# The last stage's product with both halves of w_out as one 512-column matmul, the second sum at eviction, and another order of the first stages' instructions

## The chip, the cores and the metric

The kernel runs on one core of one Trainium2 chip. The metric is the device time of one execution in microseconds; lower is better. Several executions are timed, and their median is given. One more execution is recorded by the profiler.

## The reference

Attention of 2048 tokens (4 x 8 heads, 512 tokens of width 64) with 32 state rows a head, in both directions, then two feed-forward layers over the 2176 rows. Everything is float32.

```python
def _attn_ref(x, state):
    scores = scale * np.matmul(x, state.transpose(0, 1, 3, 2))
    a = softmax(scores); xread = np.matmul(a, state)
    scores2 = scale * np.matmul(state, x.transpose(0, 1, 3, 2))
    a2 = softmax(scores2); sread = np.matmul(a2, x)
    return np.concatenate([xread, sread], axis=2)

def _moe_ref(x, w_in, w_out):          # 2304 x 512, 512 x 2048, 2048 x 512
    h = x @ w_in
    g = np.where(h >= 1, h, np.where(h <= -1, 0.0, (h + 1) ** 2 / 4.0))
    return g @ w_out

def _moe2_ref(x, w_a, w_b, w_out):     # 512 x 1536 twice, 1536 x 512
    return (x @ w_a * (x @ w_b)) @ w_out
```

(softmax stands here for the maximum, exponential and sum of the reference, cut.)

## The kernel before

**Precision.** TensorE multiplies in a format that holds fewer bits than float32. Most operands are therefore split into a high half, a copy by ScalarE (`hi_of`, line 351), and a low half, a subtraction by VectorE (`split`, lines 358 to 362). A product of two split operands takes three matmuls: high x high, high x low, low x high (`three`, line 377). `mms` (line 364) issues them, all under line 371.

**Stages.** The first (`phase_one`, line 1332) does the attention and the first layer's h = x @ w_in. The softmaxes are taken in groups of heads; the state is multiplied into w_in first (`w_steps`, line 650, matmuls under line 660 into the banks 6 and 7, "upper"), and the softmax weights then multiply the result in 64 units of six 512-column matmuls (`h_mm`, line 799; unit t is row f of w_in's columns for the heads' group j). `gate` (line 775) applies the activation and a store writes g to DRAM. The weights come from DRAM as 8-byte numbers; `conv_steps` (line 390) turns them into float32 with a copy (line 423), a ScalarE conversion (line 346) and a VectorE join (line 434). The second stage (`b_steps`, line 952) multiplies g by w_out in three chunks of tokens. The third (`ab_run`, line 1131) forms a * b. The last stage multiplies p = a * b by the second layer's w_out, called u here.

**The last stage.** 128 tokens are done plainly (`o_plain`, line 1250), the other 2048 in eight runs of 256 (`o_run`, line 1267). A run is one step of Strassen and Winograd's scheme: seven products of half-size blocks in place of eight. A block of p is 128 tokens by 6 rows f of 128; a block of u is 6 rows f of 128 by HC = 256 columns. `sp` splits a block of p into one of eight slots (`aslot`), after sums and differences of blocks by VectorE (`v_sum`, line 900). `product` (line 1282) issues 6 x 3 matmuls of 256 columns into the first half of a bank; products 6, 7 and 4 add onto the bank of product 1, and 3 onto that of 5. `post` (from `sums`, line 858) evicts the bank behind each product: for 1, 5, 6 and 4 a ScalarE copy into the output block (`act`, line 346), for 2, 3 and 7 a VectorE addition to it (`tt`, line 356). The order of products on TensorE is 1, 7 of the run before, 5, 2, 4 of the run before, 6, 3; the last run ends with 6, 7, 3, 4. The halves of u lie one behind the other (`uv`, line 1215).

**The order of the instructions** is written by a planner (`Flow`, line 20). `op` records each instruction in the order of its creation, with the engines that may run it, a cost, and what it reads and writes. `order` (line 85) walks forward in its own time and gives each engine the ready instruction with the earliest due time (`late`). TensorE's instructions are taken in the order of creation (`chain`), except those marked `loose`, which may run when they are ready. A bank counts as taken by whoever reads or writes it. DMAs are issued on SP's queue in the planner's order.

Of the kernel before, what the change touches and what calls it, by code (L numbers as in the profile page):

```python
# [16 lines left out]
DRAM = bass.MemoryType.DRAM  # L17


class Flow:  # L20
# [13 lines left out]
    def __init__(self):  # L34
        self.ops = []
        self.last = {}
        self.readers = {}
        self.loose = set()
        self.gate = None
        self.hold = None  # L40
        self.row = None
        self.rush = 0.0
        self.port = set()
        self.hurry = {}

# [39 lines left out]
    def order(self):  # L85
# [32 lines left out]
        late = [x - self.hurry[i] for i, x in enumerate(late)]  # L118
        free = dict.fromkeys(self.LAT, 0.0)
# [15 lines left out]
        for _ in range(n):  # L135
# [40 lines left out]
            for s in after[i]:  # L176
                left[s] -= 1
                when[s] = max(when[s], free[e] if (e,) == (*ops[s][0],) and not ops[i][3] else fin[i])
                if not left[s]:
                    offer(s)  # L180
# [6 lines left out]
def attention_then_two_mlps(  # L187
# [189 lines left out]
    def three(w, x):  # L377

        return [(w[0], x[0]), (w[0], x[1]), (w[1], x[0])]
# [266 lines left out]
    def w_state(*args):  # L646
        for f in w_steps(*args):
            f()

    def w_steps(b, n, f0=0, f1=4):  # L650
# [4 lines left out]
        def emit(e):  # L655
            for j in range(4):
# [17 lines left out]
                loose=b == 0 and n > 0,  # L674
# [540 lines left out]
    def uv(i, h):  # L1215
        return V2("R0", USL[i] + 4 * UF * HC * h, UF, HC, HC)
# [50 lines left out]
    def o_run(t0, final=False):  # L1267
# [12 lines left out]
        post = sums(*bk, HC, (o0.sub(0, HC), o0.sub(HC, HC), o1.sub(HC, HC), o1.sub(0, HC)))  # L1280

        def product(i):
            u = [uv(i, h) for h in range(2)]

            def pairs():
                out = []
                for f in range(UF):
                    out += three([v()[:, f, :] for v in w[i]], [v()[:, f, :] for v in u])
                return out

            mms(bk[TO[i]], HC, pairs, i in "125", True, 3 * UF, regs(*w[i], *u), i in "3674")
            post[i]()
# [39 lines left out]
    def phase_one():  # L1332
# [39 lines left out]
        for b, (soft, tr, read, after) in enumerate(TIMES):  # L1372
# [3 lines left out]
            if b < 3:  # L1376
                if b:
                    PLAN.setdefault(16 * b - 5, []).append((st_load, b + 1))
                PLAN[soft].append((lambda b: (a_load(2 * b), a_load(2 * b + 1)), b + 1))
                PLAN.setdefault(after, []).extend([(b_qk, b + 1), (b_soft, b + 1)])  # L1380
        nv = 0
        for t in range(4 * F1):
# [8 lines left out]
            if j < 3 and f % 4 == 3:  # L1391
                w_state(j + 1, f // 4)
# [102 lines left out]

    order = flow.order()
# [81 lines left out]
```

## Time and profile before

| | |
|---|---|
| median of the runs | 720.42 us (719.61, 720.42, 723.85) |
| profiled execution | 719.44 us, its span on the core 717.3 us |
| TensorE busy | 699.2 us, 97% of the span, 4818 matmuls |
| VectorE busy | 559.3 us, 78% |
| ScalarE busy | 424.8 us, 59% |
| GpSimd busy | 97.3 us, 14%, all in the first stage |
| granted clock, mean | 0.998 |

Times in the rows are microseconds from the start of the span. PE is TensorE's matmuls, PEld its weight loads, DVE VectorE, ACT ScalarE, POOL GpSimd, SP the queue that issues DMAs. A tile's name stands without its number: `bank` is a bank of PSUM, `upper` the banks 6 and 7 together, `lower` 4 and 5, `f`, `fs`, `r` and `rh` are regions of SBUF. A matmul's recorded duration is longer than the time until the next one starts, since matmuls overlap.

### The profile page before, as it was taken

What the parts mean: (1) busy time and instruction counts of PE and PEld (TensorE: products, weight loads), DVE (VectorE), ACT (ScalarE), POOL (GpSimd) and SP (SyncE); (2) the same over time, 40 slices, a digit from 0 to 9 for tenths busy, and PEclk for the clock granted to TensorE, in tenths of its full rate; (3) what the DMA queues carried; (4) which work ended last, traced back from release to release, by engine and by line L of the source; (5) the groups of instructions that cost most, each with busy time, mean ns of one, the idle gap of its engine ahead of it and who ended that gap; (6) DMA issues with size and microseconds to landing.
All of it is one profiled execution on the core that took longest, in us unless ns stands there. A gap on an engine that the chain in (4) does not pass through costs nothing.

```text
span 717.3 us, 12235 instructions
## 1 busy us (share of the span) xinstructions
PE 699.2 (97%) x4818; PEld 655.4 (91%) x4818; DVE 559.3 (78%) x701; ACT 424.8 (59%) x625; POOL 97.3 (14%) x72
## 2 busy tenths in 40 slices
PE   7799999999999999999999999999999999999997
PEld 5456667989899999999999999999999999999997
DVE  6888879988998687899899786655636798987760
ACT  4787989797544446666566675655425535544440
POOL 3346555573100000000000000000000000000000
PEclk9999999999999999999999999999999999999999
DMA  9867967497466157143425767454541248454201
GB/s 346 357 214 245 357 236 272 149 349 250 147 200 242 35 162 219 50 141 138 133 99 203 226 203 243 157 167 135 183 163 42 87 150 279 127 188 136 87 30 44
DMA packets 75449, 128.92 MB, mean 180 GB/s; under 512 B 5632, under 2 KB 51200, under 8 KB 75392
## 3 DMA queue, kind: packets, MB, share of 16 engines
q1 hardware_dynamic: 75392, 128.15, 53.1%
q8 instruction: 37, 0.61, 0.4%
q14 instruction: 20, 0.16, 0.1%
HBM read 84.87 MB, written 43.25 MB: 179 GB/s over the span
## 4 chain that ended last, share of the span: by engine, by line
PE 82%; DVE 7%; DMA 5%; ACT 2%; issue 2%; POOL 1%; SPq 0%; DVEq 0%; POOLq 0%; ACTq 0%
PE bank L371 76%; DMA f<-in_w_dram 2%; PE bank L829 2%; DVE rh L356 2%; DMA p_d<-f 1%; DMA f<-p_d 1%; PE upper L660 1%; DVE r L356 1%; PE lower L758 1%; PE bank L853 1%; ACT f L346 1%; DVE fs L434 1%; DVE fs L549 1%; DVE fs L793 1%; ACT rh L346 0%
## 5 line engine op out<-in xcount | busy, mean ns | idle before, releaser
L371 PE MATMUL bank<-rh,r 128*128 128x352 f32 (+2 forms) x1398 | 223.5, 316 | 2.6 <-DVE rh L356 2.1
L371 PEld LDWEIGHTS bank<-rh,r 128*128 128x128 f32 x1398 | 215.8, 189 | 4.6 <-DVE rh L356 3.0
L371 PE MATMUL bank<-r,r 128*128 128x368 f32 (+1 forms) x960 | 156.1, 315 | 0.0
L346 ACT ACTIVATE f<-bank 128x368 f32<-128x368 f32 (+3 forms) x183 | 82.4, 453 | 119.3 <-PE bank L371 118.3
L371 PEld LDWEIGHTS bank<-r,r 128*128 128x128 f32 x960 | 147.9, 188 | 0.0
L346 ACT ACTIVATE rh<-f 128x736 fp32r<-128x736 f32 (+5 forms) x120 | 100.7, 846 | 77.7 <-PE bank L371 61.3
L356 DVE TENSOR_TENSOR rh<-f,rh 128x736 fp32r<-128x736 f32 (+5 forms) x120 | 120.2, 1014 | 26.1 <-ACT rh L346 25.6
L356 DVE TENSOR_TENSOR f<-bank,f 128x368 f32<-128x368 f32 (+2 forms) x168 | 85.6, 516 | 69.0 <-PE bank L371 64.0
L371 PE MATMUL bank<-r 128*128 128x512 f32 (+1 forms) x582 | 122.1, 362 | 2.8 <-ACT r L346 1.1
L371 PEld LDWEIGHTS bank<-r 128*128 128x128 f32 x582 | 95.5, 191 | 28.5 <-issue 5.1
L346 ACT ACTIVATE r<-f 128x768 fp32r<-128x768 f32 (+6 forms) x85 | 80.0, 952 | 40.8 <-PE bank L371 17.6
L356 DVE TENSOR_TENSOR r<-f,r 128x768 fp32r<-128x768 f32 (+6 forms) x85 | 91.9, 1090 | 15.7 <-ACT r L346 15.6
L371 PE MATMUL bank<-rh 128*128 128x352 f32 (+2 forms) x564 | 93.3, 318 | 0.5 <-DVE f L356 0.5
L904 DVE TENSOR_TENSOR f<-f 128x256 f32<-128x256 f32 (+7 forms) x108 | 85.8, 811 | 6.3 <-DMA f<-p_d 5.2
L371 PEld LDWEIGHTS bank<-rh 128*128 128x128 f32 x564 | 88.4, 189 | 1.4 <-issue 0.7
L371 PE MATMUL bank<-r,rh 128*128 128x368 f32 (+1 forms) x480 | 80.3, 315 | 0.0
L371 PEld LDWEIGHTS bank<-r,rh 128*128 128x128 f32 x480 | 74.3, 188 | 0.0
L346 ACT ACTIVATE f<-f 128x1024 fp8e5<-128x1024 f32 (+1 forms) x43 | 47.8, 1120 | 2.2 <-POOL f L423 2.0
L421 ACT ACTIVATE f<-f 128x512 fp8e5<-128x512 fp8e5 (+1 forms) x29 | 29.5, 1018 | 24.5 <-DMA f<-in_w_dram 18.4
L434 DVE SCALAR_TENSOR_TENSOR f<-f 128x1024 uint32<-128x1024 uint32 (+1 forms) x34 | 34.9, 1027 | 5.9 <-ACT f L346 5.8
L779 ACT ACTIVATE f<-bank,half 128x512 f32<-128x512 f32 x40 | 27.1, 686 | 8.1 <-PE bank L371 4.4
L793 DVE SCALAR_TENSOR_TENSOR f<-f,bank 128x512 f32<-128x512 f32 x40 | 26.3, 675 | 6.6 <-POOL f L788 4.0
(65 smaller groups left out, 425.9 us busy)
## 6 DMA issues: line engine op xcount, KB each, us to landing
f<-in_w_dram SPq DMA_DIRECT2D x25, 1024.0 KB, 6.2
f<-g_d SPq DMA_DIRECT2D x36, 368.0 KB, 5.5
f<-p_d SPq DMA_DIRECT2D x17, 768.0 KB, 5.0
g_d<-f SPq DMA_DIRECT2D x40, 256.0 KB, 4.3
f<-in_w_dram SPq DMA_DIRECT2D x18, 512.0 KB, 3.9
p_d<-f SPq DMA_DIRECT2D x48, 184.0 KB, 2.1
g_d<-fs SPq DMA_DIRECT2D x28, 256.0 KB, 3.6
f<-g_d SPq DMA_DIRECT2D x16, 352.0 KB, 4.5
```

What stands on the lines that cost most here:

```text
L346: lambda e: nc.scalar.activation(dst(), src(), func, **{k: (v() if callable(v) else v) for k, v in kws.items()}),
L356: op({"DVE": t_tt(n)}, lambda e: nc.vector.tensor_tensor(dst(), a(), b(), alu), rd, wr, port=port)
L371: nc.tensor.matmul(o, w, x, start=first and k == 0, stop=last and k == n - 1, skip_group_check=onto)
L421: nc.scalar.activation(to(), of(), AF.Copy, saturate=False)
L434: lambda e: nc.vector.scalar_tensor_tensor(out(U32), words_of(1, U32)(), 5, z(U32), ALU.logical_shift_right, ALU.bitwise_or),
L549: op({"DVE": 1.25}, lambda e: nc.vector.transpose(t1(), wide["lower"]), both, regs(t1))
L660: nc.tensor.matmul(banks[ab[q]][o : o + NS, :cols].rearrange("p (f x) -> p f x", x=P), st[q]()[64 * h : 64 * h + 64, NS * j : NS * j + NS] ...
L758: nc.tensor.matmul(banks[4][64 * e2 : 64 * e2 + 64, o : o + NS], xn()[:, c * 256 + p * 128 + e2 * 64 : c * 256 + p * 128 + (e2 + 1) * 64], ...
L779: lambda e: nc.scalar.activation(g(), h(), AF.Relu, bias=half[:, 0:1], scale=0.5),
L793: lambda e: nc.vector.scalar_tensor_tensor(g(), g(), 1.0, h(), ALU.min, ALU.max),
L829: nc.tensor.matmul(banks[b][:, P * i : P * i + P], w[:, P * c : P * c + P], xs()[:, P * c : P * c + P], start=c == 0, stop=c == 3,)
L904: lambda e: eng(e).tensor_tensor(dst(), a(), b(), alu),
```

## The change

In the last stage the two halves of u are laid side by side, so that a row f holds 512 columns: 256 of the high half and 256 of the low half. A product multiplies the high half of p by all 512 in one matmul, which fills a whole bank, and the low half of p by the first 256. The bank's upper 256 columns then hold high x low, and the eviction adds them: a ScalarE copy or a VectorE addition for the first half as before, and a VectorE addition for the second half, for each product.

In the first stage the products of state and w_in for the later groups of heads are created at other places (`AHEAD`), and all of them are loose. The planner takes numbers off the due times of 27 instructions (`NUDGE`, named by their number in the order of creation; a negative one makes it later), and two of them lose one of their engines.

```diff
+NUDGE = {
+    2: (2.5,), 3: (11,), 52: (11.5,), 58: (-12.5,), 62: (52.5,), 64: (53,), 65: (362,), 69: (-3.5,), 83: (-2,),
+    89: (-3,), 110: (4.5,), 137: (13, "POOL"), 163: (5.5,), 188: (-13,), 219: (-8.5,), 304: (7.5,), 328: (6, "ACT"),
+    1010: (32.5,), 1011: (5.5,), 1091: (-2.5,), 1103: (-1,), 1124: (-11.5,), 1138: (-6,), 1188: (-3.5,),
+    1211: (2.5,), 2330: (-4.5,), 2365: (9,),
+}
...
         late = [x - self.hurry[i] for i, x in enumerate(late)]
+        single = [len(e) == 1 for e, _, _, _ in ops]
+        for i, (x, *off) in self.nudge.items():
+            late[i] -= x
+            ops[i] = ({e: t for e, t in ops[i][0].items() if e not in off}, *ops[i][1:])
...
-                when[s] = max(when[s], free[e] if (e,) == (*ops[s][0],) and not ops[i][3] else fin[i])
+                when[s] = max(when[s], free[e] if single[s] and e in ops[s][0] and not ops[i][3] else fin[i])
...
-                loose=b == 0 and n > 0,
+                loose=b > 0 or n > 0,
...
     def uv(i, h):
-        return V2("R0", USL[i] + 4 * UF * HC * h, UF, HC, HC)
+        return V2("R0", USL[i] + 4 * HC * h, UF, 2 * HC, HC)
+
+    def uboth(i):
+        return V2("R0", USL[i], UF, 2 * HC, 2 * HC)
...
-        post = sums(*bk, HC, (o0.sub(0, HC), o0.sub(HC, HC), o1.sub(HC, HC), o1.sub(0, HC)))
+        c11, c12, c22, c21 = o0.sub(0, HC), o0.sub(HC, HC), o1.sub(HC, HC), o1.sub(0, HC)
+        post = {
+            "1": (0, c11, True),
+            "2": (1, c11, False),
+            "5": (2, c22, True),
+            "6": (0, c12, True),
+            "3": (2, c12, False),
+            "7": (0, c22, False),
+            "4": (0, c21, True),
+        }
+
+        def put(x, v, new):
+
+            def half(k):
+                return lambda: banks[bk[x]][:, HC * k : HC * k + HC]
+
+            for k in range(2):
+                if new and not k:
+                    act(v, half(k), HC, AF.Copy, [bank(bk[x])], regs(v))
+                else:
+                    tt(v, half(k), v, ALU.add, HC, [bank(bk[x])] + regs(v), regs(v))
 
         def product(i):
-            u = [uv(i, h) for h in range(2)]
+            b, first = bk[TO[i]], i in "125"
 
-            def pairs():
-                out = []
+            def emit(e):
                 for f in range(UF):
-                    out += three([v()[:, f, :] for v in w[i]], [v()[:, f, :] for v in u])
-                return out
-
-            mms(bk[TO[i]], HC, pairs, i in "125", True, 3 * UF, regs(*w[i], *u), i in "3674")
-            post[i]()
+                    hi, lo = (v()[:, f, :] for v in w[i])
+                    u = uboth(i)()[:, f, :]
+                    nc.tensor.matmul(banks[b], hi, u, start=first and not f, stop=False, skip_group_check=True)
+                    nc.tensor.matmul(
+                        banks[b][:, :HC], lo, u[:, :HC], start=False, stop=f == UF - 1, skip_group_check=True
+                    )
+
+            op({"PE": UF * (t_mm(512) + t_mm(HC))}, emit, regs(*w[i], *(uv(i, h) for h in range(2))), [bank(b)])
+            put(*post[i])
...
+        AHEAD = {7: [(1, 0)], 11: [(1, 1)], 15: [(1, 2)], 19: [(1, 3)], 22: [(2, 0)], 26: [(2, 1)], 30: [(2, 2)], 34: [(2, 3)], 38: [(3, 0)], 42: [(3, 1)], 45: [(3, 2)], 47: [(3, 3)]}
...
-            if j < 3 and f % 4 == 3:
-                w_state(j + 1, f // 4)
+            for b, n in AHEAD.get(t, ()):
+                w_state(b, n)
...
+    flow.nudge = NUDGE
     order = flow.order()
```

## Rows read from the trace of the kernel before

**Rows 1.** The page: span, and each engine's busy time, share and instructions.
```profile
span 717.3 us, 12235 instructions
...
PE 699.2 (97%) x4818; PEld 655.4 (91%) x4818; DVE 559.3 (78%) x701; ACT 424.8 (59%) x625; POOL 97.3 (14%) x72
```

**Rows 2.** Stretch; busy us (instructions) of PE, PEld, DVE, ACT, POOL; clock, DMA, GB/s.
```profile
20.00:30.00 10.00, 6.10 (x59) 3.21 (x60) 9.10 (x13) 7.95 (x13) 3.09 (x2) 0.89 1.02 408
...
28.30:31.50 3.20, 3.20 (x9) 2.48 (x9) 2.52 (x3) 3.20 (x7) 1.23 (x1) 0.54 1.02 406
...
40.00:60.00 20.00, 17.94 (x189) 11.10 (x189) 19.75 (x22) 15.86 (x21) 10.22 (x8) 1.00 0.75 241
```

**Rows 3.** Timeline: start, duration, instructions merged, count, idle time before and releaser.
```profile
54.36 1.09 PE L660 MATMUL upper<-fs 64*32 64x512 f32 x16 [1.26 <-DVE r L356]
...
185.60 2.28 PE L371 MATMUL bank<-rh,r 128*128 128x368 f32 x12 [0.75 <-DVE rh L356]
```

**Rows 4.** Busy time by stretch in the last stage, columns as in rows 2.
```profile
620.00:640.00 20.00, 20.00 (x171) 20.00 (x170) 18.39 (x26) 10.55 (x17) 0.00 (x0) 1.00 0.52 171
...
680.00:700.00 20.00, 20.00 (x171) 20.00 (x170) 13.64 (x17) 8.26 (x13) 0.00 (x0) 1.00 0.11 41
```

**Rows 5.** Timeline of TensorE: 512-column matmuls, first stage; 256-column ones, last stage.
```profile
121.38 0.50 PE L371 MATMUL bank<-r 128*128 128x512 f32 x1
...
121.71 5.40 PE L371 MATMUL bank<-r 128*128 128x512 f32 x23
...
126.72 0.39 PE L371 MATMUL bank<-r 128*128 128x512 f32 x1
...
698.21 4.42 PE L371 MATMUL bank<-r,r 128*128 128x256 f32 x36
...
702.47 2.32 PE L371 MATMUL bank<-rh 128*128 128x256 f32 x18
```

**Rows 6.** VectorE's instructions from 603.0 to 633.8 us: count, busy us, mean ns, idle.
```profile
L356 DVE TENSOR_TENSOR r<-f,r 128x768 fp32r<-128x768 f32 x13 | 11.9, 951 | 0.0
...
L356 DVE TENSOR_TENSOR rh<-f,rh 128x768 fp32r<-128x768 f32 x6 | 5.7, 952 | 0.2 <-ACT rh L346 0.2
L356 DVE TENSOR_TENSOR f<-bank,f 128x256 f32<-128x256 f32 x7 | 2.7, 417 | 0.0
```

**Rows 7.** Timeline: two evicting additions in a row.
```profile
626.51 0.75 DVE L356 TENSOR_TENSOR f<-bank,f 128x256 f32<-128x256 f32 x2
```

**Rows 8.** Timeline where run 1 of the last stage begins.
```profile
602.32 0.96 DVE L904 TENSOR_TENSOR f<-f 128x768 f32<-128x768 f32 x1 [2.83 <-DMA f<-p_d]
...
604.20 1.97 PEld L371 LDWEIGHTS bank<-rh,r 128*128 128x128 f32 x16 [0.26 <-DVE r L356]
```

**Rows 9.** Timeline of the end: product 7 after product 6, and the last copy.
```profile
706.95 0.38 ACT L346 ACTIVATE f<-bank 128x256 f32<-128x256 f32 x1 [1.74 <-PE bank L371]
...
707.39 2.39 PE L371 MATMUL bank<-rh,r 128*128 128x256 f32 x18 [0.47 <-ACT f L346]
...
714.03 0.38 ACT L346 ACTIVATE f<-bank 128x256 f32<-128x256 f32 x1 [6.70 <-PE bank L371]
```

**Rows 10.** Timeline from 20 to 28 us, VectorE's order ahead of the steady matmuls.
```profile
20.62 1.78 DVE L423 COPY f<-f 128x1024 uint8<-128x1024 uint8 x1
...
21.19 0.45 ACT L346 ACTIVATE r<-upper 128x128 fp32r<-128x128 f32 x2 [0.50 <-PE upper L660]
...
22.30 0.47 DVE L356 TENSOR_TENSOR r<-upper,r 128x128 fp32r<-128x128 f32 x2
...
22.69 1.21 DVE L695 TENSOR_REDUCE fs<-lower 128x2 f32<-128x1024 f32 x1
...
23.82 2.33 DVE L434 SCALAR_TENSOR_TENSOR fs<-f 128x1024 uint32<-128x1024 uint32 x2
...
26.07 0.74 DVE L356 TENSOR_TENSOR r<-upper,r 128x256 fp32r<-128x256 f32 x2
...
26.87 1.13 PE L660 MATMUL upper<-fs 64*32 64x512 f32 x16 [2.46 <-DVE r L356]
```

More of the change, by code (lines that the diff above doesn't have):

```diff
@@ L44, in __init__ @@
         self.hurry = {}
+        self.nudge = {}
     def op(self, engs, emit, rd=(), wr=(), size=0, loose=False, port=False):
```

## The prediction

> **What bounds the kernel now.** I read the page first: TensorE is busy for 97% of a span of 717.3 us, VectorE for 78%, and the chain that ended last runs over TensorE for most of its length [rows 1]. Busy time says little here, because matmuls overlap; what counts is the time from start to start, and where TensorE waits. So I next read the table of busy time by stretch. In the first stages TensorE is busy only 6.10 of 10 us from 20 to 30 us, its granted clock is 0.54 from 28.3 to 31.5 us (nearly all at the lower of its two levels, 1.2 GHz, where it was idle much of the time before), and from 40 to 60 us VectorE is busy 19.75 of 20 us [rows 2]. The timeline then shows single waits of TensorE: 1.26 us at 54.36, where the product of state and w_in for the next pair of heads stands in a fixed place and its two banks still wait for a VectorE subtraction, and 0.75 us at 185.60, one of two such within 4 us [rows 3]. From 190 us to the last stage TensorE streams almost without a gap. In the last stage VectorE has little room at first (18.39 of 20 us busy from 620 to 640) and much later (13.64 of 20 from 680 to 700) [rows 4]. So the last stage is paid in matmul time, as long as VectorE keeps up, and the first stages in waits.
>
> **The matmuls of the last stage.** Eight runs of seven products stream, for each of the six rows f of a product, 3 x 256 columns; after the change 512 + 256, the same 768. What is saved is the fixed part of one matmul, 8 x 7 x 6 = 336 times. The 36 matmuls of 256 columns from 698.21 to 702.47 stand 4.26/36 = 0.1183 us apart. Of 512 columns the trace has rows in the first stages: from 121.71 to the start of the 23rd at 126.72, 5.01/22 = 0.2277 us; with the one before, at 121.38, 5.34/23 = 0.2322 [rows 5]. So a row f goes from 3 x 0.1183 = 0.3549 to 0.2277 + 0.1183 = 0.3460, 8.9 ns less: 336 x 0.0089 = 3.0 us. Bounds: with 0.2322 it is 4.4 ns and 1.5 us; if one whole fixed part goes (0.1183 less 256 columns at 2.4 GHz, 0.1067, so 11.6 ns), 3.9 us. I take 3.0, since the 0.2277 comes from a steady stretch as the last stage is. Zero, where 512 columns cost just two matmuls of 256 (0.2366), is a rival below.
> The Trainium skill speaks against this (TensorE: Matmul & The Clock Gate, Back-to-back issue gap): a warm matmul costs its columns at 2.4 GHz and some 2.5 ns; by that, 336 fewer matmuls would give an estimated 0.8 us. The trace disagrees so far: 0.1183 and 0.2277 us lie 11.6 and 14.4 ns above the column time.
>
> **The second sum at the eviction.** Each product now ends with two evictions of 256 columns in place of one: the high half's product with the low half of w_out lies in the bank's upper 256 columns and VectorE adds it. The four products that ScalarE copied (1, 5, 6, 4) get an add behind the copy, the three that VectorE added (2, 3, 7) a second add: 56 more adds. One takes 0.417 us [rows 6], but two in a row 0.75 us [rows 7], so 0.33 to 0.42 each, 18.5 to 23.5 us of VectorE in all. What hides them is VectorE's idle time and its lead. From 603.0 to 633.8 us it made 13 + 6 = 19 low-half splits, beside the sums and 7 adds, with almost no idle time [rows 6]; TensorE used up 30.8/2.13 = 14 products in that time (2.13 us is half of the 4.26 above), two of them split before. So VectorE gained 7 products, some 7 x 30.8/19 = 11 us of its time. Fifteen more adds there take 5.0 to 6.3 us: the lead grows more slowly but does not go. From 680 on 10 more adds (4.2 us) fit in 6.4 us of idle time per 20. I charge 0.3 us for single late evictions; a bank's next product comes two or more products (4 us) later, but for the end of the last run.
> If the cover is gone, TensorE waits for splits as it does once now: at 604.20 its weight load waits 0.26 us for VectorE, whose sum began 2.83 us late because a load of p had not landed [rows 8]. That load also sets the start of run 1, so what the five products of run 0 before it save (5 x 6 x 8.9 ns = 0.27 us) is lost there: +0.3 us.
> **The end.** In the last run product 7 follows product 6 in the same bank: TensorE waits 0.47 us for ScalarE's copy, and the last instruction before the store is a copy of 0.38 us behind product 4 [rows 9]. Both now have an add behind them that needs the copy: 0.42 each, and a hand-over, which was 0.06 us from the copy's end at 707.33 to TensorE's start at 707.39: +0.47 twice, +0.9 us. No work covers either.
> Last stage: -3.0 + 0.3 + 0.3 + 0.9 = -1.5 us. The strided layout of the split w_out (steps of 512) moves no instruction and its 256-column pieces stay whole: nothing.
>
> **The order of the first stages.** Two edits, and none of them issues a DMA of its own. First, the twelve products of state and w_in for later heads are created up to four units later and are now all free to start when their banks are free, where they held a fixed place in TensorE's order. The wait at 54.36 [rows 3] is of that kind: TensorE can run the next unit instead. I take -1.0 of its 1.26 us, since VectorE is full there [rows 2] and part comes back as another wait; its bounds are 0 and -1.26.
> Second, 27 numbers shift due times. Counting creations in the code, 62 and 64 are the low subtractions of the second state product, moved ahead by 53 us; 52 is the copy for w_in rows 4 and 5, by 11.5; 65 is the maximum for the second softmax, by 362. In the trace that copy holds VectorE from 20.62 for 1.78 us, the two subtractions come after it at 22.30 though ScalarE had written their other operand by 21.64, then the maximum (1.21 us) stands in front of the two joins at 23.82, and behind those the subtractions at 26.07 release the matmuls at 26.87 that waited 2.46 us [rows 10]. Putting the subtractions first is worth 22.30 - 21.64 = 0.7 us, the maximum elsewhere 1.2 us less what it delays; I take -1.7 for both (bounds 0 and -1.9). The copy behind them is needed for the fourth unit only, some 5 us later. SP's queue changes little: the two first loads were first already. Two of the numbers also bind one instruction each to a single engine; I take nothing for it, since it moves work of 1 to 2 us between engines and removes none. The stretch at half clock right after costs half of 3.2 us x 0.92, some 1.5 us; it follows the idle time before it and may go with it (-1.5) or stay; I leave it in. Of the two waits from 185.60 on, and smaller ones that later numbers (1010 to 1211, third chunk) touch, I take -0.8 of 1.5, both ends 0 and -1.5.
> First stages: -1.7 - 1.0 - 0.8 = -3.5 us; ends 0 and -6.2 (1.9 + 1.3 + 1.5 + 1.5).
>
> **Sum.** The profiled execution took 719.44 us. 719.44 - 1.5 - 3.5 = 714.4. It lay 0.98 below the median of the runs, and below all three; I add half of that, 0.5, to each case: 714.9, said as 715.0.
>
> **Rivals** (from 719.44, with the 0.5).
> A. All first waits and the half clock go: -1.5 - 6.2, so 712.2; with the upper bound of the matmul term 711.3. For: the waits are VectorE's order, not its total, before 40 us. Against: 19.75 of 20 us from 40 to 60.
> B. The order gains nothing because VectorE's work is only permuted: 719.44 - 1.5 + 0.5 = 718.4.
> C. The change does not do what it says: 512 columns cost two of 256, nothing is saved, and adds and end remain (+1.5 with the 0.3 for run 1 left out: +1.2): 719.44 + 1.2 - 3.5 + 0.5 = 717.6. Against: [rows 5]. The rule of the Trainium skill above (same page and section) comes close to it: its estimated 0.8 us would make this case 716.8.
> D. VectorE is late in runs 1 to 3: the lead of 11 us was partly splits made early by putting adds off, and adds can be put off less now. Each of some 14 products would wait as at 604.20, about 0.3 us: +4.2, so 719.1. It decides when adds and the lost lead exceed 11 us.
> E. Slower: the copy of 1.78 us pushed behind the subtractions is late for the fourth unit; TensorE idles at 30 us instead of 26, and a second 3.2 us at half clock follows. +1.78 + 1.6 in place of -3.5, since the later stages start late too: 719.44 - 1.5 + 3.4 + 0.5 = 721.8. It decides when w_in's join comes after 31 us. Against: it has 5 us.
>
> **Numbers.** Forecast 0.37, A 0.20, B 0.14, C 0.10, D 0.12, E 0.07. Within 1% (7.2 us, about what a measurement of this kernel tells from no change) means 713.2 to 727.6. Faster by more: nearly all of A and a quarter of the forecast, whose own range is 712.5 to 717: 0.28. Slower by more: only E at double its price, 0.03. Same: 0.69. The range 710.0 to 721.0 goes 1.3 us under A's end, for waits too short to be listed here, and leaves out most of E.
>
> **What would show it.** Right: 336 fewer matmuls; rows of 512 columns in the last stage about 0.228 us apart from start to next start; 80 VectorE adds from the banks in place of 24; an idle time of about 0.9 us before product 7; the start of the steady stream at 26 instead of 28 us; no wait at 54. Wrong: waits of TensorE's weight loads for VectorE between 604 and 645 (D), the lower clock twice (E), a product of the last stage still 2.13 us long (C).

## The result, and the profile after

The median went from 720.36 us (719.61 to 723.85) to 713.0 us (711.8 to 713.18): a ratio of 0.9885, with an interval of 0.9851 to 0.9919. That is 7.4 us, where 715.0 and 5.4 us were forecast. The profiled execution of the changed kernel took 713.18 us, its span 711.3 us, 6.0 us less than that of before.

In the new numbering the lines up to the last stage stand 13 lines lower (L371 is now L384, L356 is L369, L346 is L359, L423 is L436, L434 is L447, L660 is L673, L758 is L771, L793 is L806, L904 is L917). The last stage's matmuls are L1325, of 512 columns, and L1326, of 256.

The page of after, its span and its engines (before: [rows 1]):

```profile
span 711.3 us, 11604 instructions
...
PE 695.4 (98%) x4482; PEld 638.2 (90%) x4482; DVE 575.0 (81%) x759; ACT 420.5 (59%) x620; POOL 104.6 (15%) x75
...
L369 DVE TENSOR_TENSOR f<-bank,f 128x368 f32<-128x368 f32 (+2 forms) x224 | 108.4, 493 | 69.9 <-PE bank L384 57.0
```

336 matmuls are gone (4818 to 4482). The last row is the group of VectorE additions from the banks; it holds 224. The same group on the page of before holds 168, so 56 were added, as the code says:

```profile
L356 DVE TENSOR_TENSOR f<-bank,f 128x368 f32<-128x368 f32 (+2 forms) x168 | 85.6, 516 | 69.0 <-PE bank L371 64.0
```

Busy time by stretch of after; the columns are those of [rows 2], and the stretches those of [rows 2, 4]:

```profile
20.00:30.00 10.00, 5.20 (x40) 1.99 (x40) 9.51 (x15) 8.04 (x12) 2.56 (x2) 0.84 1.02 408
40.00:60.00 20.00, 20.00 (x137) 13.02 (x136) 18.93 (x25) 16.57 (x26) 10.25 (x8) 1.00 0.83 290
...
620.00:640.00 20.00, 20.00 (x117) 17.50 (x116) 18.79 (x29) 8.93 (x15) 0.00 (x0) 1.00 0.33 107
680.00:700.00 20.00, 20.00 (x115) 17.28 (x113) 17.59 (x29) 7.59 (x13) 0.00 (x0) 1.00 0.08 31
```

TensorE lost time between 20 and 30 us (5.20 us busy after 6.10) and gained it from 40 to 60 (20.00 after 17.94). In the two stretches of the last stage it has no idle time although VectorE is busier (18.79 us after 18.39, and 17.59 after 13.64). Its weight loads, PEld, are busy 17.50 and 17.28 of 20 us there, after 20.00 and 20.00.

**Where the time came from.** The first 256-column matmul of the last stage starts at 578.86 us where it started at 583.56: 4.70 us are won before the last stage. From there to the start of the last matmul it is 128.45 us after 130.16, 1.71 less; from there to the end of the span 4.01 after 3.57, 0.44 more. 4.70 + 1.71 - 0.44 = 6.0. So most came from the order, not from the matmuls.

These are two executions, and executions differ. The eight runs of the last stage begin at 593.08 us in before and at 588.38 in after. In the six other profiled kernels below with the new order and its whole first-stage table (e0, e2, e5, e6, e7, e10) they begin at 586.70 to 588.84. So the order is worth 4.2 to 6.4 us by the traces, and 4.70 lies near the lower end. (e1, which has the order of before, begins them at 594.14.)

The 4.70 us are mostly waits of TensorE. Its idle time up to 580 us, added up over the stretches, fell from 14.22 to 11.28 us, by 2.9. A wait costs more than its idle time shows: before product 7 it made the product 1.09 us longer than the median (3.197 - 2.111) where its idle time is 0.93, since a recorded matmul reaches into the gap behind it. The part of the 4.70 that neither explains was not traced. Between 20 and 190 us the waits with a releaser fell from eleven to five.

The wait view of TensorE from 20 to 190 us, first of before and then of after (columns: group, releaser, us in total, times, longest):

```profile
PE upper L660 <- DVE r L356: 4.1, 3, 2.5
PE bank L371 <- DVE rh L356: 1.5, 2, 0.8
PE upper L660 <- DVE fs L434: 1.3, 1, 1.3
PE bank L371 <- DVE fs L793: 0.6, 1, 0.6
...
```

```profile
PE upper L673 <- DVE r L369: 4.6, 2, 4.4
PE lower L771 <- ACT fs L359: 0.7, 1, 0.7
PE bank L384 <- ACT r L359: 0.6, 1, 0.6
PE bank L384 <- DVE r L369: 0.4, 1, 0.4
```

The two waits for a split's low half, the pair from 185.60 on [rows 3], are gone, and so is that at 54.36. The product of state and w_in still waits, and in one place longer than before.

That place is the start. TensorE, VectorE and one row of ScalarE of after there (columns: start, us; before: [rows 10]):

```profile
20.36 0.49 DVE L369 TENSOR_TENSOR r<-upper,r 128x128 fp32r<-128x128 f32 x2
20.75 1.23 DVE L447 SCALAR_TENSOR_TENSOR fs<-f 128x1024 uint32<-128x1024 uint32 x1
...
23.80 0.42 DVE L369 TENSOR_TENSOR r<-upper,r 128x256 fp32r<-128x256 f32 x1
24.13 0.68 DVE L714 TENSOR_SCALAR fs<-fs 128x2 f32<-128x2 f32 x1
24.29 0.36 ACT L359 ACTIVATE r<-upper 128x256 fp32r<-128x256 f32 x1
24.87 0.75 DVE L436 COPY f<-f 128x1024 uint8<-128x1024 uint8 x1
25.51 1.21 DVE L447 SCALAR_TENSOR_TENSOR fs<-f 128x1024 uint32<-128x1024 uint32 x1
26.64 0.41 DVE L369 TENSOR_TENSOR r<-upper,r 128x256 fp32r<-128x256 f32 x1
...
27.11 1.96 PE L673 MATMUL upper<-fs 64*32 64x512 f32 x16 [4.41 <-DVE r L369]
29.00 3.58 PE L384 MATMUL bank<-r 128*128 128x512 f32 x12
```

The subtractions come at 20.36 instead of 22.30, as the prediction wanted. But the last subtraction that releases the next state product now stands behind a small instruction, a copy and a join, and ends at 27.05. ScalarE had written its other operand by 24.65. So the 2 us won ahead of it are lost again, and the stream begins at 29.00 instead of 27.93.

### The profile page after: what moved, and what is told of

Read it like the earlier page. It is cut to its first block, busy times and chain, and to the rows that moved or that the text cites. A ratio compares the mean times of both kernels' runs of the same rounds, so it can differ in the third digit from the quotient of the medians.

```text
span 711.3 us, 11604 instructions
## 1 busy us (share of the span) xinstructions
PE 695.4 (98%) x4482; PEld 638.2 (90%) x4482; DVE 575.0 (81%) x759; ACT 420.5 (59%) x620; POOL 104.6 (15%) x75
## 4 chain that ended last, share of the span: by engine, by line
PE 89%; DVE 4%; DMA 4%; ACT 1%; issue 1%; POOL 0%; DVEq 0%; POOLq 0%; ACTq 0%
PE bank L384 67%; PE bank L1325 11%; PE bank L1326 6%; PE bank L842 2%; PE upper L673 2%; DMA f<-in_w_dram 2%; DMA g_d<-fs 1%; PE lower L771 1%; DMA f<-g_d 1%; PE bank L866 1%; DVE fs L447 1%; ACT f L359 1%; DVE f L436 0%; DVE r L369 0%; PE lower L539 0%
## 5 line engine op out<-in xcount | busy, mean ns | idle before, releaser
L384 PE MATMUL bank<-rh,r 128*128 128x352 f32 (+2 forms) x1074 | 181.8, 326 | 1.0 <-DVE rh L369 1.0
L384 PEld LDWEIGHTS bank<-rh,r 128*128 128x128 f32 x1074 | 176.3, 188 | 1.9 <-DVE rh L369 1.6
L359 ACT ACTIVATE f<-bank 128x368 f32<-128x368 f32 (+3 forms) x183 | 82.7, 454 | 141.8 <-PE bank L384 90.2
L369 DVE TENSOR_TENSOR f<-bank,f 128x368 f32<-128x368 f32 (+2 forms) x224 | 108.4, 493 | 69.9 <-PE bank L384 57.0
L359 ACT ACTIVATE rh<-f 128x736 fp32r<-128x736 f32 (+5 forms) x120 | 100.3, 846 | 71.6 <-PE bank L384 63.4
L369 DVE TENSOR_TENSOR rh<-f,rh 128x736 fp32r<-128x736 f32 (+5 forms) x120 | 119.0, 1001 | 22.2 <-ACT rh L359 21.8
L384 PE MATMUL bank<-r,r 128*128 128x368 f32 x672 | 120.6, 330 | 0.0
L384 PEld LDWEIGHTS bank<-r,r 128*128 128x128 f32 x672 | 113.1, 188 | 0.1
L384 PE MATMUL bank<-r 128*128 128x512 f32 (+1 forms) x438 | 102.0, 385 | 2.4 <-ACT r L359 1.2
L369 DVE TENSOR_TENSOR r<-f,r 128x768 fp32r<-128x768 f32 (+6 forms) x85 | 94.1, 1121 | 10.2 <-ACT r L359 9.8
L384 PEld LDWEIGHTS bank<-r 128*128 128x128 f32 x438 | 77.5, 190 | 27.3 <-issue 7.5
L359 ACT ACTIVATE r<-f 128x768 fp32r<-128x768 f32 (+6 forms) x85 | 80.1, 954 | 26.7 <-DVE f L917 11.6
L917 DVE TENSOR_TENSOR f<-f 128x256 f32<-128x256 f32 (+6 forms) x106 | 83.3, 804 | 1.9 <-DMA f<-p_d 1.2
L384 PE MATMUL bank<-rh 128*128 128x352 f32 (+1 forms) x456 | 79.4, 327 | 0.0
L384 PEld LDWEIGHTS bank<-rh 128*128 128x128 f32 x456 | 75.1, 188 | 0.9 <-DVE f L369 0.4
L384 PE MATMUL bank<-r,rh 128*128 128x368 f32 x336 | 62.4, 330 | 0.0
L384 PEld LDWEIGHTS bank<-r,rh 128*128 128x128 f32 x336 | 56.8, 188 | 0.0
L359 ACT ACTIVATE f<-f 128x1024 fp8e5<-128x1024 f32 (+1 forms) x43 | 48.1, 1121 | 1.8 <-DVE f L436 0.8
L434 ACT ACTIVATE f<-f 128x512 fp8e5<-128x512 fp8e5 (+1 forms) x28 | 28.1, 1003 | 20.2 <-DMA f<-in_w_dram 15.5
L1325 PE MATMUL bank<-rh,r 128*128 128x512 f32 x108 | 38.6, 396 | 0.9 <-DVE f L369 0.9
L447 DVE SCALAR_TENSOR_TENSOR f<-f 128x1024 uint32<-128x1024 uint32 (+1 forms) x34 | 34.0, 1000 | 6.3 <-ACT f L359 6.1
L1325 PE MATMUL bank<-r,r 128*128 128x512 f32 x96 | 34.2, 396 | 0.0
```

Of the source, the lines that this page charges most:

```text
L359: lambda e: nc.scalar.activation(dst(), src(), func, **{k: (v() if callable(v) else v) for k, v in kws.items()}),
L369: op({"DVE": t_tt(n)}, lambda e: nc.vector.tensor_tensor(dst(), a(), b(), alu), rd, wr, port=port)
L384: nc.tensor.matmul(o, w, x, start=first and k == 0, stop=last and k == n - 1, skip_group_check=onto)
L434: nc.scalar.activation(to(), of(), AF.Copy, saturate=False)
L447: lambda e: nc.vector.scalar_tensor_tensor(out(U32), words_of(1, U32)(), 5, z(U32), ALU.logical_shift_right, ALU.bitwise_or),
L917: lambda e: eng(e).tensor_tensor(dst(), a(), b(), alu),
```

## The experiments

Twelve kernels ran, in three groups, each beside runs of the kernel before on its chip. The differences are between medians, each against the before of its own group (720.15, 719.95 and 720.71 us).

| run | median us | against before | ratio, interval |
|---|---|---|---|
| e1_last_only | 719.28 | -0.87 | 0.9985 (0.9974 to 0.9996) |
| e2_order_only | 713.55 | -6.60 | 0.9906 (0.989 to 0.9921) |
| e3_no_nudge | 718.64 | -1.51 | 0.9977 (0.9963 to 0.999) |
| e4_loose_only | 722.93 | +2.78 | 1.0029 (1.0014 to 1.0044) |
| e0_after_again | 712.9 | -7.05 | 0.9903 (0.9889 to 0.9916) |
| e5_three_narrow | 714.22 | -5.73 | 0.9925 (0.9911 to 0.9938) |
| e6_no_second_sum | 711.46 | -8.49 | 0.9882 (0.9868 to 0.9895) |
| e7_end | 710.61 | -9.34 | 0.9872 (0.9858 to 0.9885) |
| e8_first_328 | 713.66 | -7.05 | 0.9893 (0.9874 to 0.9913) |
| e9_first_110 | 720.67 | -0.04 | 0.9995 (0.9981 to 1.0009) |
| e11_not_loose | 724.36 | +3.65 | 1.0042 (1.0028 to 1.0057) |
| e10_one_more | 712.27 | one execution | |

### The two halves of the change: e1_last_only, e2_order_only

The first is the kernel before with the edit of the last stage alone; the second is the changed kernel with the last stage of before, and without the table's numbers 2330 and 2365, which point into the last stage. Of e1, against the kernel before:

```diff
-        return V2("R0", USL[i] + 4 * UF * HC * h, UF, HC, HC)
+        return V2("R0", USL[i] + 4 * HC * h, UF, 2 * HC, HC)
...
+                    nc.tensor.matmul(banks[b], hi, u, start=first and not f, stop=False, skip_group_check=True)
```

> The kernel before with the last stage's edit alone: 512-column matmuls and the second sum, the order of the first stages as before. Theory: the two edits add up, and the last stage gives what its stretch gave in the changed kernel, 1.3 us (starts 1.7 us closer together, the end 0.4 us longer): 719.1 against 720.4, first matmul of 256 columns at 583.3 as before. Rival 1: the last stage needs the other order too, and VectorE comes late in runs 1 to 3 without it: 720.4 or more, with waits of TensorE between 604 and 640. Rival 2: the full 3.0 us of the prediction less 1.2: 718.6 or less, products of 2.08 us throughout.

> The changed kernel with the last stage of before (three matmuls of 256 columns, one eviction; the two numbers of the last stage left out of the table). Theory: the order is worth 4.7 us before the last stage, as the first 256-column matmul of the changed kernel stood 4.7 us earlier: 715.7, and that start at 578.6. Rival: the order was worth more in time than the spans show, 6 us or more (714.4 or less), since the medians fell by 7.4 and the spans by 6.0.

The last stage alone is worth 0.9 us, the order alone 6.6. 0.9 + 6.6 = 7.5, and both together gave 7.4 and, again, 7.1: the halves add up, and the order is the larger. In e1 the products of the last stage have nearly the same lengths as in after; from the start of its first product to that of its last matmul the last stage takes 119.03 us, 1.61 less than in before.

### What merging the matmuls is worth: e5_three_narrow

The 512-column matmul is cut in two again; the layout, the banks and all evictions of the change stay.

```diff
-                    nc.tensor.matmul(banks[b], hi, u, start=first and not f, stop=False, skip_group_check=True)
+                    for k in range(2):
+                        nc.tensor.matmul(
+                            banks[b][:, HC * k : HC * k + HC], hi, u[:, HC * k : HC * k + HC],
+                            start=first and not f and not k, stop=False, skip_group_check=True,
+                        )
```

> The changed kernel with its wide matmul cut in two: high x high and high x low each as 256 columns into the two halves of the bank, and both evictions as in the changed kernel. So only the merging of two matmuls is undone. Theory: a product goes back from 2.11 to 2.14 us, 56 x 0.03 = 1.6 us slower than the changed kernel run beside it. Rival 1 (the prediction): 3.0 us slower. Rival 2: the merging is worth nothing and the product stays at 2.11, so what made products shorter is that the bank's halves are written apart.

It took 1.3 us more than after in the same group (714.22 against 712.9). By the trace, the 52 products ahead of the last three sum to 111.22 us in e5, as in before apart from its one stall, and to 109.36 in e10_one_more, whose last stage is that of after: 1.86/52 x 56 = 2.0 us. So merging is worth 1.3 us by the medians and 2.0 by the trace, not 3.0.

The intervals say which price was off. In before and in e5 a 256-column matmul stands on average 119 ns after the one before it; in after the 512-column one takes 233.0 ns and the 256-column one 117.5. By the 52 products a row f goes from 356.5 to 350.5, 6.0 ns less, where 8.9 were counted.

A merged matmul also saves a weight load: PEld has 4818 instructions in e5, as in before, and 4482 in after, and from 620 to 640 us it is busy 20.00 of 20 us in e5. Whether the 6.0 ns belong to the matmul or to its weight load no run tells apart.

Two products of after, first a fast one and then a slow one (start, us):

```profile
638.92 0.39 PE L1325 MATMUL bank<-r,rh 128*128 128x512 f32 x1
639.15 0.28 PE L1326 MATMUL bank<-r,rh 128*128 128x256 f32 x1
...
641.00 0.39 PE L1325 MATMUL bank<-r,rh 128*128 128x512 f32 x1
```

```profile
647.32 0.39 PE L1325 MATMUL bank<-r,r 128*128 128x512 f32 x1
647.55 0.28 PE L1326 MATMUL bank<-r,r 128*128 128x256 f32 x1
647.66 0.40 PE L1325 MATMUL bank<-r,r 128*128 128x512 f32 x1
647.90 0.28 PE L1326 MATMUL bank<-r,r 128*128 128x256 f32 x1
...
649.43 0.39 PE L1325 MATMUL bank<-r 128*128 128x512 f32 x1
```

The fast product takes 2.08 us, 641.00 less 638.92; the slow one 2.11, its 512-column matmuls alternately about 0.23 and 0.24 us long. The stretch of [rows 5], with 0.2277, was like the fast kind.

### What decides fast or slow: e10_one_more

One more matmul is put among those that warm TensorE at the start; all later instructions of TensorE shift by one.

```diff
-            for _ in range(n):
+            for _ in range(n + (n == WARM)):
```

> The changed kernel with one more 128-column matmul among the eleven that warm TensorE up at the start, in idle time; every other instruction as it was, so that TensorE's instructions lie one matmul further on and no operand has moved. A product of the last stage takes 2.08 or 2.12 us, in the same sequence in four kernels. If the place of the operands decides, the sequence stays (2.081, 2.105, 2.12, 2.12, 2.12, 2.095, 2.08, 2.111 from the start of run 0); if the place in the instruction stream decides, it shifts or changes. The time itself stays within 0.3 us of the changed kernel's.

The product lengths stay as they were, in the same order (2.081, 2.105, 2.12, 2.12, 2.12, 2.095, ... in after 2.081, 2.105, 2.12, 2.12, 2.12, 2.096). Only the seventh differs, 2.080 after 2.166, and e0, the changed kernel once more, has 2.080 there as well. The lengths also repeat in e1, whose earlier instructions stand in another order. So the pattern goes with the product, and a shift by one instruction does not move it.

The expectation put it down to where the operands lie. No run moves all of them, but e5 moves one. Products of three 256-column matmuls have a pattern of their own, 2.149, 2.127, 2.130, 2.133, 2.132, ... in before, and e5 repeats it to 1 ns in the products ahead of the last three, apart from the one stall of before, though its u lies in another way and its second matmul writes another half of the bank. So it is not the layout of u. The place of the split blocks of p and the values that are multiplied are left, and neither was varied.

### What the second sum costs: e6_no_second_sum

The 56 additions of the upper half are left out, so the product high x low is missing from the output; the numbers 2330 and 2365 are left out too.

```diff
-            for k in range(2):
+            for k in range(1):
```

> The changed kernel without the second sum: the 56 additions of the upper halves are left out, so high x low is missing in the output (and the two due times of the last stage are left out). Theory: only the wait ahead of product 7 in the last run (0.48) and the add behind the last copy (0.42) lie on the path, so 0.9 us faster than the changed kernel. Rival: VectorE, 88 to 99 per cent busy in the last stage, holds TensorE up in other places too: 1.5 us or more faster.

The end of e6 (start, us), TensorE and ScalarE, against that of after:

```profile
699.43 0.51 PE L1325 MATMUL bank<-rh,r 128*128 128x512 f32 x1 [0.47 <-ACT f L359]
...
706.01 0.38 ACT L359 ACTIVATE f<-bank 128x256 f32<-128x256 f32 x1 [6.64 <-PE bank L1326]
```

```profile
700.13 0.38 ACT L359 ACTIVATE f<-bank 128x256 f32<-128x256 f32 x1 [0.25 <-PE bank L1326]
700.55 0.42 DVE L369 TENSOR_TENSOR f<-bank,f 128x256 f32<-128x256 f32 x1 [0.41 <-ACT f L359]
...
701.03 0.50 PE L1325 MATMUL bank<-rh,r 128*128 128x512 f32 x1 [0.93 <-DVE f L369]
...
707.62 0.38 ACT L359 ACTIVATE f<-bank 128x256 f32<-128x256 f32 x1 [7.11 <-PE bank L1326]
708.04 0.42 DVE L369 TENSOR_TENSOR f<-bank,f 128x256 f32<-128x256 f32 x1 [1.61 <-ACT f L359]
```

Without the additions the wait before product 7 is 0.47 us, exactly as in before [rows 9], and with them 0.93. The last-stage stretch of e6 is 0.45 us shorter than that of e0, and its end 0.46; the 52 products ahead of the last three sum to 109.36 us in both. So of 56 additions two cost time, 0.9 us together, and the other 54 nothing that shows. The median fell by 1.4; the remaining 0.5 lies ahead of the last stage, where this execution also lacks a wait of 0.70 us at 98.57 that after has (e0: 0.64). Up to 575 us each engine's instructions stand in the same order in both traces, so nothing in the profile ties that part to the additions; its cause is open.

### Taking the end's 0.9 us back: e7_end

The last run's order becomes 1, 7 of the run before, 5, 6, 2, 4 of the run before, 7, 3, 4, so that product 2 and product 4 of the run before stand between 6 and 7. The last product is done in three 256-column matmuls a row, onto a bank whose upper half a ScalarE copy has put into the output ahead of it, so one addition follows. Numbers 2330 and 2365 are left out.

```diff
+            if final and i == "4":
...
+                act(c21, lambda: banks[bk[0]][:, HC:], HC, AF.Copy, [bank(bk[0])], regs(c21))
+                mms(bk[0], HC, pairs, False, True, 3 * UF, regs(*w[i], *u), True)
+                tt(c21, lambda: banks[bk[0]][:, :HC], c21, ALU.add, HC, [bank(bk[0])] + regs(c21), regs(c21))
+                return
```

> The changed kernel with another end of the last run: the products stand 1, 7, 5, 6, 2, 4, 7, 3, 4, so that one or two others lie between two that use the same bank; the upper half of the bank is copied before the last product, that product is three matmuls of 256 columns, and one addition ends it. Theory: the wait of 1.18 us ahead of product 7 goes and the last eviction is 0.4 us shorter: 1.5 us faster than the changed kernel. Rival: the operand of product 6 is needed a product earlier, VectorE has it late, and a new wait of 0.5 us or more stands there.

The end of e7 (start, us):

```profile
701.44 0.38 ACT L359 ACTIVATE f<-bank 128x256 f32<-128x256 f32 x1 [2.67 <-DVE f L369]
...
702.35 2.32 PE L384 MATMUL bank<-rh,r 128*128 128x256 f32 x18
...
704.78 0.42 DVE L369 TENSOR_TENSOR f<-bank,f 128x256 f32<-128x256 f32 x1 [1.11 <-PE bank L384]
```

TensorE has no wait left in the last stage. Its stretch is 117.69 us from the first product of run 0 to the last matmul, in e0 118.82, and the end 3.68 after 4.02: 1.5 us less. The copy lies beside product 3, and only an addition of 0.42 us follows the last matmul. With 710.61 us this is faster than both kernels; of the 2.3 us under e0 another 0.8 lies ahead of the last stage and is not explained by the edit.

### The table of numbers: e3_no_nudge, e8_first_328, e9_first_110

The changed kernel with an empty table; with the numbers up to 328 only; and up to 110 only.

```diff
-    flow.nudge = NUDGE
+    flow.nudge = {}
```

> The changed kernel with an empty table of due times; the products of state and w_in are still loose and at their new places. Theory: loose products take away the waits from 40 to 60 us (2.1 us), the table takes away those at 184 and 188 (2.1 us): 713.0 + 2.6 = 715.6. Rival 1: the table does nothing, 713.0. Rival 2: the table does it all, 713.0 + 4.7 = 717.7.

> The changed kernel with only the numbers of the first stage (2 to 328) in the table of due times; those of the second stage's third chunk (1010 to 1211) and of the last stage (2330, 2365) are out. Theory: with no numbers the waits of 0.5, 0.8 and 0.6 us at 279, 297 and 327 stood, in the changed kernel 0.6 and 0.7 at 275 and 318 stand: the late numbers are worth 0.6 us or less, so 712.9 to 713.5. Rival: the late numbers carry much of the 5.7 us that the table is worth: 715 or more.

> The changed kernel with only the first eleven numbers of the table (2 to 110), which touch the start up to 30 us. Theory: the start is not where the time went, since the fourth unit starts no earlier than before (34.2 against 33.2 us); the numbers 137 to 328 take away the waits of 1.6 and 2.1 us at 50 and 84: 717 to 718, near the kernel without the table (718.6). Rival (the prediction): the start is worth 1.7 us or more of it, and its order decides what comes after: 715.5 or less.

Without the table 1.5 us of the 7 are left (e3), less than any of the three expectations had. The numbers up to 328 give all of it, 7.05 (e8), so the later ones, from 1010 on, are worth nothing that the medians show. The numbers up to 110 alone give 0.04, which is 1.5 us worse than no table (e9; a larger step than was expected of it). So the numbers 137 to 328 are worth 7.0 us on top of the start's numbers, and the start's numbers alone cost 1.5. No run has the numbers 137 to 328 without those of the start, so whether the start's still cost beside them is not shown.

TensorE's waits in the timeline of e3 (start, us), and then the wait view of e9 from 20 to 190 us:

```profile
26.08 1.09 PE L673 MATMUL upper<-fs 64*32 64x512 f32 x16 [2.47 <-DVE r L369]
...
52.14 1.09 PE L673 MATMUL upper<-fs 64*32 64x512 f32 x16 [1.49 <-DVE r L369]
...
87.21 0.97 PE L384 MATMUL bank<-r 128*128 128x512 f32 x3 [2.02 <-DVE fs L806]
```

```profile
PE upper L668 <- DVE r L364: 4.6, 2, 4.3
PE bank L379 <- DVE f L801: 1.6, 3, 0.9
PE bank L379 <- DVE fs L801: 0.9, 2, 0.6
PE bank L379 <- POOL r L577: 0.7, 1, 0.7
```

With no table the state product waits 2.47 us at 26.08, as it did in before [rows 10], and 1.49 at 52. With the start's numbers the longest such wait is 4.3 us, about that of after, and the one at 52 is gone, but eight smaller ones of 0.2 to 0.9 us, five of them for the gate's instructions (L801 in e9), take its place. With all numbers up to 328 the long one stays and the small ones go. Which of the numbers 137 to 328 do this was not taken apart.

The wait of 2.02 us in e3 costs more than itself. Behind it the granted clock falls once more, which before and after do not show there (columns as in [rows 2]):

```profile
88.50:92.00 3.50, 3.50 (x10) 2.76 (x9) 3.46 (x6) 2.35 (x4) 1.04 (x1) 0.51 0.66 249
```

At 0.51 nearly all of the 3.5 us is at the lower level, 1.2 GHz, and half of it, an estimated 1.7 us, is lost: a part of what the table is worth. The two runs of e3 with a mean granted clock of 0.998 are its fastest (716.33 and 716.50 us, the other ten 717.22 to 721.29), which fits.

### The loose state products: e4_loose_only, e11_not_loose

e4 is e3 with the state products created at the old places, so that only their being loose is left of the order's change. e11 is the changed kernel with its new places and its table, but the state products of the later groups fixed in TensorE's order as before.

In e4:

```diff
-            for b, n in AHEAD.get(t, ()):
-                w_state(b, n)
+            if j < 3 and f % 4 == 3:
+                w_state(j + 1, f // 4)
```

In e11:

```diff
-                loose=b > 0 or n > 0,
+                loose=b == 0 and n > 0,
```

> As the one without the table, and the products of state and w_in are created where they were before; they are only loose. Theory: a loose product runs when its banks are free and its eviction when it is due, so the place of creation does not matter: within 0.5 us of the one without the table. Rival: the later places are what relieves VectorE from 40 to 60 us: 1 to 2 us slower than the one without the table, with a wait of TensorE at 50 to 55 us.

> The changed kernel with the products of state and w_in in a fixed place again, at the new places of creation and with the whole table. Theory: the table was made for loose ones, and a fixed product waits for its banks as at 54 us in the kernel before: 1 to 3 us slower than the changed kernel, with a wait of TensorE ahead of such a product. Rival: loose products only cost (the one with loose products alone was 2.8 us slower than before, with TensorE held for 5 us by one that came too early), and the later places do the work: no slower than the changed kernel.

TensorE's waits, first of e4 and then of e11 (start, us):

```profile
31.84 1.96 PE L673 MATMUL upper<-fs 64*32 64x512 f32 x16 [4.51 <-DVE r L369]
...
56.30 1.09 PE L673 MATMUL upper<-fs 64*32 64x512 f32 x16 [2.44 <-DVE r L369]
```

```profile
56.32 1.09 PE L673 MATMUL upper<-fs 64*32 64x512 f32 x16 [2.60 <-DVE r L369]
...
132.67 1.09 PE L673 MATMUL upper<-fs 64*32 64x512 f32 x16 [2.03 <-DVE r L369]
```

Loose alone makes it slower: e4 lies 3.65 us above e1, from which it differs by that alone (+2.78 against -0.87). The trace shows the wait. The planner's order is written for its own times; a state product that it places early waits while VectorE still reads its banks, 4.51 us at 31.84, and the matmuls behind it, which show no wait of their own, start only after it. Creating them up to four units later takes 4.3 us off (e3 against e4). And with the new places and the table, but fixed, the kernel is 10.7 us slower than with them loose (e11's +3.65 against e0's -7.05), where 1 to 3 were expected; of that an estimated 1.7 us goes to a second stretch at the lower clock behind the wait at 132.67 (0.61 from 133 to 137.4 us, that is 3.4 us at 1.2 GHz, of which half is lost). So loose products alone cost time, and so do the new places and the table without them. Loose products and the table are both needed for the 6.6 us; that the new places are needed too is shown only without the table (e3 against e4), since no run has the table at the old places.

## Why the prediction was right, and where its steps were not

The time lay in its range, 2.0 us under the forecast, and its own condition for "faster" (over 1%, the ratio at 0.9885) came about, if barely, since the interval reaches 0.9919; to this it gave 0.28. The number owes something to luck: the start came out on the wrong side, and waits that went further than counted made up for it. Step by step:

- **What bounds it.** Right. The last stage was paid in matmul time with VectorE keeping up, the first stages in waits.
- **The matmuls, -3.0.** Mis-sized: -2.0 by the trace, 1.3 by e5's medians, still within the bounds of 1.5 to 3.9 by the one and just out by the other. The step that failed took 0.2277 us from a steady stretch of the first stage; the last stage has 0.2330. Rival C is out, since e5 is slower than after. The rule of the Trainium skill that the prediction set against the rows (TensorE: Matmul & The Clock Gate, Back-to-back issue gap), which that section gives for a matmul by itself and not for a stream with weight loads, gave an estimated 0.8 us; the trace's 2.0, 6.0 ns for each matmul saved, is more than its 2.5, and less than the forecast's 8.9.
- **Late evictions and the start of run 1, +0.3 each.** Neither came. From 620 to 640 us VectorE had 1.2 us of idle time left and TensorE none; of the wait of 0.26 us at 604.20 [rows 8] some 0.09 is left in after, where the seventh product takes 2.166 us and 2.080 in e0 (in e1 some 0.2: two products there take 2.182 and 2.193). Rival D is out: 54 of the 56 additions cost nothing (e6). One reading of this step was off: 19 splits against 14 products is a gain of 5 in that time, and 7 is the lead at its end, two having been split before; the argument stands with 5.
- **The end, +0.9.** Right: 0.47 to 0.93 us before product 7, and 0.44 more from the last matmul to the end. e6 and e7 both take it away.
- **The last stage, -1.5.** -1.71 + 0.44 = -1.3 in the spans, -0.9 alone (e1). Two errors offset: a matmul term 1.0 too large, and 0.6 of charges that did not come.
- **The wait at 54.36, -1.0.** It went in full: idle time from 40 to 60 us fell by 2.06. Loose alone would not have done it; e4 has 2.44 us at 56.30. With the later places as well, but no table, 1.49 us are left at 52.14 (e3); with the table's first eleven numbers the wait is gone (e9). So the step named the right wait and left out a cause: the table is needed.
- **The start, -1.7.** The wrong sign. The subtractions came 1.9 us sooner, and the stream 1.07 later. The step ended at the first subtractions and did not ask what VectorE would do between them and the last one: two copies and three joins. In before GpSimd made two such copies between 20 and 28 us, in after none. e9 agrees, where these numbers alone are 1.5 us worse than none, and the stream begins at 28.41 where it begins at 27.10 in e3. The half-clock stretch stayed, as the sum had it.
- **Waits at 185.60 and the others, -0.8.** Under-sized: from 160 to 200 us TensorE was busy 38.49 us before and 40.00 after, so all 1.5 went, and the 0.57 at 80 to 100 and 0.38 at 100 to 120 became 0.70 and 0. The later numbers, to which the prediction gave a part of it, added nothing to the median (e8). The pair at 185.60 is gone without any table too (e3) and with fixed products (e11), while e4, at the old places, keeps one of 0.74 us: by these runs it went with the later places.
- **The order, -3.5.** Mis-sized: -4.70 in the profiled executions, -6.6 by e2's medians. This is where the forecast's 2.0 us went, and A was the rival nearest to it, by its time (712.2) but not by its way: it had the half clock and the start's wait gone, and both stayed.
- **Rivals B and E.** B is out, since the order alone gained 6.6 us (e2). E's mechanism, a late release and a second half-clock stretch, shows in e11 after the wait of 2.03 us at 132.67, and in e3 after that of 2.02 at 87.21. In after it did not happen.

## What to carry to other kernels

A gain from reordering can't be read off one wait: list what the engine that releases it does until the last release, not until the first, and test the parts together as well as singly, since loose alone cost 3.7 us and the three parts gave 6.6. A matmul interval should come from the stage in which it will run, over many products. Work added on an engine with idle time was free here except where the next step had nothing else to run: 54 of 56 additions cost nothing, the two at the end 0.9 us, and moving work round them gave 1.5 us in the last stage, about what the merge gave (1.3 to 2.0).

## What the runs showed of the hardware

The intervals of the same 512-column matmul were 0.23 us in some products and alternately 0.23 and 0.24 in others, in the same sequence in every kernel with this last stage. One more instruction ahead of them (e10) did not move it, and another layout of u (e5 beside before) did not change the pattern of the 256-column products. The cause is open.

The granted clock falls to its lower level of 1.2 GHz early in each execution, after TensorE was idle for much of the time (from 15 to 20 us it is busy 2.83 of 5 us in before and 2.96 in after), but for different lengths: about 3.4 us in before and after, 6.8 us in e0, 10.2 us in e1. Its stretch in e1, in e0 and in after (columns as in [rows 2]):

```profile
20.00:30.50 10.50, 8.23 (x58) 3.74 (x59) 9.40 (x14) 7.85 (x13) 3.33 (x3) 0.51 1.03 410
```

```profile
26.00:33.00 7.00, 6.38 (x27) 3.75 (x28) 6.02 (x10) 5.49 (x6) 1.90 (x2) 0.51 0.94 372
```

```profile
26.50:30.50 4.00, 3.39 (x20) 1.49 (x21) 3.60 (x8) 3.22 (x4) 0.00 (x0) 0.57 1.03 411
```

The first stages of e1 hold the same instructions in the same order as those of before, and e0 is after once more, so the length does not come from the edit. Runs of one kernel lie 1 to 5 us apart. Of the runs of before beside e1, the eleven with a mean granted clock of 0.993 took 720.3 us on average and the seven with 0.998 took 720.5, so the mean clock alone does not set its runs apart.
